# Score bias of the first two batches added by a bf16 matmul instead of on VectorE, with a table that shifts 100 event priorities

## The chip, the cores and the metric

The kernel runs on one core of a Trainium2 chip. The metric is device time in microseconds (us) of one execution, as the median of several runs. Engines are called as in the profile: PE is TensorE, DVE is VectorE, ACT is ScalarE, POOL is GpSimd, SP is SyncE, whose queue issues most of the DMAs.

## The reference: windowed attention, a 2-D Fourier transform and a two-layer network

Inputs are q, k and v of shape (8 batches, 8 heads, 576 positions, 64), and the weights w1 (512 x 2048) and w2 (2048 x 512), which arrive as 64-bit floats.

```python
scores = scale * np.matmul(q, k.transpose(0, 1, 3, 2))
bias = slopes[:, None, None] * (-np.abs(rel))[None]      # slopes 2**-(h+1), rel = position of query - position of key
mask = (rel >= 0) & (rel < 128)
attn = softmax(np.where(mask, scores + bias, -1e9))
x = np.matmul(attn, v)                                   # heads joined: (8, 576, 512)
u = x + np.real(np.fft.fft(np.fft.fft(x, axis=1), axis=2))
un = (u - mean(u)) / sqrt(var(u) + 1e-6)
out = u + np.maximum(un @ w_ch1, 0) @ w_ch2
```

## The kernel before, in words

**Pairs, groups, tiles.** Attention goes by pairs p of heads (four pairs to a batch, so p = 0 to 31). The queries of a pair lie in five tiles, which are taken in three groups (SGRP). A pair's two heads lie on partitions 0 to 63 and 64 to 127, so one head's score matmul uses 64 rows of the PE array. For each group and head a PSUM bank `sp0` or `sp1` is taken from a pool with two of each; the transposes (`turn`) take banks from the same pool.

**The first two batches** (NF = 2, p = 0 to 7) are computed with fp32 matmuls; the later ones split each number into two fp16 halves. For p < 8, `products` issues one fp32 matmul per tile and head (the profile counts each fp32 matmul as two). `spread` then runs one custom DVE instruction per tile and head (L684), which adds the table of distances `rel_sb` times the slope to the scores, writes the result `P` to SBUF and takes the row's extreme into `nb`. DVE is then done with the bank. ACT takes the exponential of `P` in place, `turn` transposes it on PE, ACT copies it out (L718), and `values` multiplies by v (L737). `weigh` divides by the row sums into `X`.

**Fillers.** `warm` (L580) issues PE matmuls whose result nobody reads: SPIN = 5 of them behind each `turn` of the first four pairs, SPIN1 = 1 behind each later one.

**Behind attention.** When all heads of batch b are in `X`, `fourier(b)` folds them on DVE (it begins with a memset of a row of `X`, L801), runs `rows`, `middle` and `cols` on PE and adds the result to `X` (`cols_add`, for j = 1, 0, 2). `norm` takes the statistics of each 128-token tile (bn_stats, L978), a power on POOL, the shift `nmr` on DVE (L983), scales on ACT and sends the result through a transposing DMA to `uT`. `ffn(b)` is the two layers (L1151 and L1173); it is written FFN(0) here for batch 0.

**Side work.** While the first batches run, the weights are loaded, rebuilt from 64-bit words (`rebias`, `join`), measured (`gram`, L466 on PE) and split in two halves (`high`, `low`, L488). `batch_scales(b)` loads a later batch's q, k and v once more into `wall` (`fetch`) to measure them.

**What sets the order.** Every event is put into a queue with a time by hand (`put`); the events are traced in the order of these times. `keep_order` then hands the traced instructions to `arrange`, a list scheduler with its own cost table: on each engine it takes the ready instruction that was traced first. That order is fixed by dependencies, so it is the order in which each engine's instructions stand.

Of the kernel before, what the change touches and what calls it, by code (L numbers as in the profile page):

```python
# [22 lines left out]
NF = 2  # L23
# [23 lines left out]
WL = (-2.569, 0.042)  # L47
PL, VL = 7.393, 1.751
FL, SA, SD, SB, SE = 1.9, 16.181, 0.696, 24.041, 1.166
DFT = 30.695  # L50
START = 47.844
PACE, T1 = (0.507, 0.514), 13.742
SPIN, GAP = 5, 1.315
SLOW = 1.476
W2A, W2D, W2B, W2E = 13.895, 0.615, 21.285, 0.518
W1D, W1B, W1E = 0.379, 11.116, 0.977
F0 = 5.97
SW = 184
SPIN1 = 1
DS, D0 = 1.0, 12  # L60
# [22 lines left out]
WIDTH = {"float32": 4, "float16": 2, "bfloat16": 2, "int32": 4, "int64": 8}  # L83
LANES = ("PE", "DVE", "Activation", "Pool", "SP")
# [28 lines left out]
def cells(a, seen):  # L113
# [4 lines left out]
    if b.tensor.name[:2] in ("fp", "sp", "pv", "pd"):  # L118
        return b.tensor.name, 0, 128, 1
# [16 lines left out]
def nanoseconds(i, lane):  # L136
# [20 lines left out]
    if lane == "Activation":  # L157
        psum = any(a.bass_ap.tensor.name[:2] in ("fp", "sp", "pv", "pd") for a in reads)
        return (58 if psum else 102) + 0.835 * n + 90 * scaled + 190 * (len(i.outs) > 1), False
# [11 lines left out]
def collect(traced):  # L171
    work, seen, last = [], {}, -1
    for at, i in enumerate(traced):
# [21 lines left out]
    writes, reads = {}, {}  # L195
    for n, it in enumerate(work):
        for (t, p0, p1, bits), w in it.uses:
            for l, real in ((writes, True),) + (((reads, False),) if w else ()):
                for m, q0, q1, other in l.get(t, ()):
                    if m != n and q0 < p1 and p0 < q1 and bits & other:  # L200
                        it.waits[m] = it.waits.get(m, False) or real
# [10 lines left out]
def arrange(work, slots):  # L212
# [31 lines left out]
    while len(order) < len(work):  # L244
        best = None
        for e in LANES:
            while now[e] or later[e]:
                t = free[e] if now[e] else max(free[e], later[e][0][0])
                while later[e] and later[e][0][0] <= t:
                    heappush(now[e], heappop(later[e])[1])  # L250
                n = now[e][0]
                t1, tag = buffers(n)
                if t1 is None:
                    held.setdefault(tag, []).append(heappop(now[e]))
                elif t1 > t:
                    ready[n] = max(ready[n], t1)
                    heappush(later[e], (ready[n], heappop(now[e])))
# [5 lines left out]
        n = heappop(now[e])  # L263
# [32 lines left out]
        for m, real in it.then:  # L296
            same = work[m].lane == e
            ready[m] = max(ready[m], end if same and (e == "PE" or not real and e != "SP") else seen + WAKE[work[m].lane])
# [14 lines left out]
def keep_order(tc, slots):  # L313
# [6 lines left out]
    order, takers = arrange(work, slots)  # L320
# [15 lines left out]
def attn_fft_ffn_kernel(  # L336
# [83 lines left out]
    def put(t, f, *a):  # L420
        heappush(queue, (t, next(order), f, a))
# [4 lines left out]

    stage = xp.tile([128, 5, DM], F32, name="X").rearrange("p a b -> p (a b)")
# [85 lines left out]
    def batch_scales(b, t0, dt):  # L513
# [6 lines left out]
        def fetch(x, fl, o, n):  # L520
# [5 lines left out]
            if b > NF:  # L526
                G.tensor_copy(box[x][1][0:1, 0:1], last[-1])
# [124 lines left out]
    def products(p, i):  # L652
        b, j = divmod(p, 4)
        if b < NF:
            prods = ((ops[p][0], ops[p][1]),)
        else:
# [3 lines left out]
        sp = banks[p, i] = [ps_s.tile([128, 512], F32, name=f"sp{e}") for e in range(2)]  # L660
        col = 0
# [10 lines left out]
    def spread(p, i):  # L672
        b, j = divmod(p, 4)
        grp, sp = SGRP[i], banks.pop((p, i))
        P = Ps[p, i] = {}
        for e in range(2):
# [114 lines left out]
    def fourier(b, t0):  # L791
# [161 lines left out]
        for j in (1, 0, 2):  # L953
# [3 lines left out]
            t += f * 0.8  # L957
        put(t0 - 0.1, lambda: uTs.__setitem__(b, []))
# [389 lines left out]
```

## Time and profile before

| What | Value |
|---|---|
| Median of 3 runs | 1042.02 us (1040.59 to 1042.19) |
| The profiled execution | 1041.73 us, span 1039.9 us |
| Mean granted TensorE clock | 0.99 of full speed |
| Busy in the span | PE 97%, DVE 73%, ACT 59%, POOL 7% |

The span runs from the first to the last instruction, and the profiled execution's time is 1.8 us longer. A share of busy time is a mean over stages with different limits. The granted clock has two levels, 1.2 GHz (0.5) and 2.4 GHz (1.0); a value between them is a stretch that held some of each.

### The profile page before, as it was taken

How to read it: one execution, taken by the hardware profiler on the slowest of the kernel's cores; microseconds unless marked ns; L12 is line 12 of the kernel's file. 1: busy time of each engine (PE TensorE's matmuls, PEld its weight loads, DVE VectorE, ACT ScalarE, POOL GpSimd, SP SyncE). 2: the span in 40 equal slices, each digit the busy share in tenths (PEclk: the TensorE clock that was granted, in tenths of full speed). 3: DMA queues.
4: the chain of work that ended last, by engine and by line, in shares of the span. 5: the costliest groups of instructions: out<-in, count | busy, mean ns of one | idle time of the engine just before them, and what ended most of it. 6: DMA issues, size and time to landing. Idle time of an engine off the chain costs nothing.

```text
span 1039.9 us, 24569 instructions
## 1 busy us (share of the span) xinstructions
PE 1006.7 (97%) x9352; PEld 730.7 (70%) x9352; DVE 761.8 (73%) x2211; ACT 609.9 (59%) x1438; POOL 73.3 (7%) x243
## 2 busy tenths in 40 slices
PE   8997799899999999999999999999999999999998
PEld 5785585575767677675767677676767776858886
DVE  5898867986784768778784768779684848987451
ACT  7897967676745566567655566667444532445230
POOL 0000001100210012000000012000000000010000
PEclk9998899999999999999999999999999999999999
DMA  9953517656553366534863376434532230011000
GB/s 365 397 187 95 127 34 197 165 105 152 148 135 87 83 154 145 142 77 121 170 136 90 81 157 146 139 80 103 111 93 33 58 70 11 11 35 39 21 3 30
DMA packets 191511, 117.86 MB, mean 113 GB/s; under 512 B 154400, under 2 KB 164128, under 8 KB 191392
## 3 DMA queue, kind: packets, MB, share of 16 engines
q1 hardware_dynamic: 190816, 114.84, 43.9%
q8 instruction: 73, 1.20, 0.5%
q10 hardware_dynamic: 576, 1.45, 0.4%
q14 instruction: 46, 0.38, 0.1%
HBM read 70.63 MB, written 9.44 MB: 77 GB/s over the span
## 4 chain that ended last, share of the span: by engine, by line
PE 66%; DVE 6%; DMA 3%; ACT 2%; issue 1%; POOL 0%; SPq 0%; ACTq 0%; DVEq 0%; POOLq 0%
PE fp L1151 28%; PE fp L1173 25%; PE fp L1088 4%; PE sp L668 3%; DMA pt<-P 2%; PE pd L871 2%; PE pd L905 1%; PE pv L742 1%; PE pv L744 1%; PE pv L743 1%; DVE hbuf L424 1%; DVE P L684 1%; DMA qr<-q_dram 0%; DVE P L424 0%; PE pd L888 0%
## 5 line engine op out<-in xcount | busy, mean ns | idle before, releaser
L1151 PEld LDWEIGHTS <-wall 128*128 128x128 f16 x3840 | 338.8, 98 | 46.2 <-issue 7.9
L1151 PE MATMUL fp<-uT,wall 128*128 128x256 f16 x3072 | 356.1, 273 | 4.5 <-DVE hbuf L424 4.0
L1173 PE MATMUL fp<-wall,hbuf 128*128 128x512 f16 x1536 | 349.1, 379 | 0.7 <-DVE hbuf L424 0.7
L1173 PEld LDWEIGHTS <-hbuf 128*128 128x128 f16 x1536 | 143.6, 98 | 161.0 <-issue 3.1
L1156 ACT ACTIVATE hbuf<-fp 128x512 f16<-128x512 f32 x144 | 85.0, 591 | 186.7 <-PE fp L1151 186.7
L424 DVE SCALAR_TENSOR_TENSOR hbuf<-fp,hbuf 128x512 f16<-128x512 f32 x144 | 98.7, 686 | 95.0 <-ACT hbuf L1156 94.4
L424 ACT ACTIVATE P<-P,nb 128x256 f32<-128x256 f32 x320 | 132.3, 477 | 13.8 <-DVE nb L684 8.2
L684 DVE CUSTOM_DVE_ANT_0 P<-sp,rg,nsl 128x256 f32<-128x256 f32 x240 | 96.2, 448 | 20.8 <-PE sp L668 15.4
L424 DVE SCALAR_TENSOR_TENSOR P<-P 128x256 f16<-128x256 f32 x240 | 83.0, 389 | 22.2 <-ACT P L697 21.6
L697 ACT ACTIVATE P<-P 128x256 f16<-128x256 f32 x240 | 80.7, 385 | 22.4 <-DMA pt<-P 18.7
L668 PE MATMUL sp<-kk,qq 64*128 64x256 f16 (+5 forms) x880 | 77.3, 287 | 4.1 <-DVE kk L424 3.0
L535 ACT ACTIVATE wall<-wall 128x512 f32<-128x512 f32 (+2 forms) x90 | 54.1, 601 | 35.6 <-DMA wall<-k_dram 17.5
L742 PE MATMUL pv<-vhs,pt 128*128 128x65 f16 x432 | 53.9, 195 | 3.9 <-DMA pt<-P 1.9
L743 PE MATMUL pv<-vl,pt 128*128 128x64 f16 x432 | 53.9, 193 | 0.0
L744 PE MATMUL pv<-vhs,pt 128*128 128x65 f16 x432 | 53.8, 193 | 0.0
L742 PEld LDWEIGHTS <-pt 128*128 128x128 f16 x432 | 41.3, 98 | 16.1 <-issue 4.6
L737 PE MATMUL pv<-vr,pt 128*128 128x65 f32 x288 | 40.7, 281 | 5.6 <-DVE X L760 5.1
L743 PEld LDWEIGHTS <-pt 128*128 128x128 f16 x432 | 40.4, 99 | 7.5
L1151 PE MATMUL fp<-wall,wall 128*128 128x128 f16 x768 | 45.0, 219 | 0.0
L737 PEld LDWEIGHTS pv<-vr,pt 128*128 128x128 f32 x288 | 37.9, 200 | 8.8 <-issue 7.1
L668 PEld LDWEIGHTS <-qq 64*128 64x128 f16 (+1 forms) x720 | 31.1, 99 | 15.4 <-issue 11.7
L744 PEld LDWEIGHTS <-pt 128*128 128x128 f16 x432 | 40.6, 97 | 0.0
(230 smaller groups left out, 1380.5 us busy)
## 6 DMA issues: line engine op xcount, KB each, us to landing
qr<-q_dram SPq DMA_DIRECT2D x32, 304.0 KB, 4.0
hbuf<-w_dram SPq DMA_DIRECT2D x16, 512.0 KB, 8.7
out_dram<-X SPq DMA_DIRECT2D x32, 256.0 KB, 2.2
wall<-v_dram SPq DMA_DIRECT2D x30, 256.0 KB, 3.0
vr<-v_dram SPq DMA_DIRECT2D x24, 320.0 KB, 3.7
kr<-k_dram SPq DMA_DIRECT2D x24, 289.0 KB, 4.4
wall<-q_dram SPq DMA_DIRECT2D x24, 256.0 KB, 3.3
wall<-k_dram SPq DMA_DIRECT2D x24, 256.0 KB, 3.0
```

Source lines behind the costliest of these rows:

```text
L424: put(now[0] + dt, lambda: f(*a, **kw))
L535: A.activation(t, t, AF.Square, accum_out=box["mx"][:, i, c:c + 1])
L668: T.matmul(sp[e][:m, col:col + n], qq[h, c0:c0 + m], keys(kk[h], ti), start=(x == 0), stop=(x == len(prods) - 1))
L684: V.tensor_tensor_reduce(pt[:m, 0:n], sp[e][:m, col:col + n], tab[:m, pc:pc + n], mul, 3.0e38, ALU.add, ALU.min, nb[:m, ti:ti + 1])
L697: A.activation(hi, P32, AF.Copy, scale=2.0 ** 14)
L737: T.matmul(pv[:, ti], pt[:, col:col + 128], ops[p][2][:, e, vc], start=first, stop=last)
L742: T.matmul(pv[:, ti], ph, vh[:, e, vc], start=first, stop=False)
L743: T.matmul(pv[:, ti, 0:D], ph, vl[:, e, vc], start=False, stop=False)
L744: T.matmul(pv[:, ti], pl, vh[:, e, vc], start=False, stop=last)
L1151: T.matmul(fp[:, i * n:(i + 1) * n], w1_ap(e, c, f), uT[:, j, c, 0:n], start=(c == 0 and p == 0), stop=(c == 3 and p == 2))
L1156: A.activation(ht[:, 0], fp, AF.Relu)
L1173: T.matmul(op, hh[f][:, a, i * 128:(i + 1) * 128], w2_ap(e, f), start=(f == 0 and p == 0), stop=(f == 15 and p == 2))
```

## The change

Seven things are changed.

- **Bias on PE.** For p < 8, `products` calls `biased`: per tile and head, a bf16 matmul of `eye` (the 128 x 128 identity times minus the head's slope) with the table `rel_sb` opens the accumulation in the bank, and the fp32 score matmul closes it. The query scale becomes a constant -0.125. `spread` calls `smallest`: DVE only takes the row minimum from PSUM (one instruction for both tiles of the middle group), and ACT takes the exponential straight from PSUM into `P`. A bank is therefore free when ACT has read it. POOL builds the eight `eye` matrices once.
- **Fillers.** SPIN goes from 5 to 1.
- **Statistics.** The first `norm` of a batch is put right behind j = 0 of `cols`, ahead of j = 2. `nmr` is allocated when it is written.
- **Loads.** `fetch` for batches from 3 on loses the POOL copy that made each load wait for the last `weigh`.
- **Scheduler.** `collect` distinguishes three kinds of dependency, and `arrange` sorts ready instructions by a rank.
- **Priorities.** The rank is the event's time plus a shift from `LATER`, a table of 100 named events (the rest have none).
- **Constants.** Some fifteen of the hand-written times change, and three are new.

```diff
-SPIN, GAP = 5, 1.315
+SPIN, GAP = 1, 1.32
...
+LATER = {
+    "W1.load.1": 0.75, "scores.(0,2)+1": 0.15, "W0.gram.3": 12.05, "W0.join.4": 2.8, "W0.gram.6": 2.1,
...
+    eye = att.tile([128, 8, 128], BF16, name="rg", bufs=2)
+    for h in range(8):
+        G.tensor_scalar(eye[:, h], ident, -2.0 ** -(h + 1), None, ALU.mult)
...
-            if b > NF:
-                G.tensor_copy(box[x][1][0:1, 0:1], last[-1])
             nc.sync.dma_start(out=box[x][1], in_=fl[:, o:o + n])
...
-            A.activation(qs, qr, AF.Copy, scale=slope_sb[:, 12 + j:13 + j])
+            A.activation(qs, qr, AF.Copy, scale=-0.125)
...
+        if b < NF:
+            biased(p, i, sp)
+            return
...
+        if b < NF:
+            smallest(p, i, sp)
+            return
...
-                tab, mul = (rel_sb, -2.0 ** -(h + 1)) if b < NF else (scs[b][2], scs[b][1][:m, h:h + 1])
-                V.tensor_tensor_reduce(pt[:m, 0:n], sp[e][:m, col:col + n], tab[:m, pc:pc + n],
-                                       mul, 3.0e38, ALU.add, ALU.min, nb[:m, ti:ti + 1])
+                V.tensor_tensor_reduce(pt[:m, 0:n], sp[e][:m, col:col + n], scs[b][2][:m, pc:pc + n],
+                                       scs[b][1][:m, h:h + 1], 3.0e38, ALU.add, ALU.min, nb[:m, ti:ti + 1])
...
+    def biased(p, i, sp):
+        j, grp = p % 4, SGRP[i]
+        o0 = PCOL[grp[-1]]
+        for ti in grp:
+            c0, pc, n = TILES[ti][0], PCOL[ti], 128 * len(TILES[ti][2])
+            for e in range(2):
+                T.matmul(sp[e][:, pc - o0:pc - o0 + n], eye[:, 2 * j + e], rel_sb[:, pc:pc + n], start=True, stop=False)
+            for e in range(2):
+                h = slice(64 * e, 64 * e + 64)
+                T.matmul(sp[e][:, pc - o0:pc - o0 + n], ops[p][0][h, c0:c0 + 128], keys(ops[p][1][h], ti),
+                         start=False, stop=True)
+
+    def smallest(p, i, sp):
+        grp, P = SGRP[i], Ps[p, i]
+        o0 = PCOL[grp[-1]]
+        for e in range(2):
+            nb = small.tile([128, 5], F32, name="nb", bufs=6)
+            if i == 1:
+                V.tensor_reduce(nb[:, 2:4], sp[e].rearrange("p (a b) -> p a b", a=2), AX.X, ALU.min)
+            for ti in grp:
+                m, o, n = TILES[ti][1], PCOL[ti] - o0, 128 * len(TILES[ti][2])
+                if i != 1:
+                    V.tensor_reduce(nb[:, ti:ti + 1], sp[e][:, o:o + n], AX.X, ALU.min)
+                pt = P[e, ti] = att.tile([128, 256], F32, name="P", bufs=PB)
+                after(0.25, A.activation, pt[:m, 0:n], sp[e][:m, o:o + n], AF.Exp, bias=nb[:m, ti:ti + 1], scale=-1.0)
...
+            if j < 1:
+                put(t - f * 0.1, norm, b, lambda: st["X"][0:2], t + f * N1)
         put(t0 - 0.1, lambda: uTs.__setitem__(b, []))
-        for i, t1 in enumerate((t - f * 0.1, t + f * 0.7)):
-            put(t1, norm, b, lambda i=i: st["X"][2 * i:2 * i + 2], t + f * (0.9 + 1.6 * i))
+        put(t + f * N2, norm, b, lambda: st["X"][2:4], t + f * N3)
```

The table and the scheduler move instructions on every engine. Two places show it. The first is PE in the second pair of heads, around the `values` of its second group (`x3` is three alike; `kk,qq` are scores, `ident,P` transposes, `vr,pt` values, `pv<-pt` fillers). Before:

```order
L668 MATMUL sp_582<-kk,qq 96x256
L715 MATMUL sp_605<-ident,P 128x128 x3
L737 MATMUL pv<-vr,pt 128x65 x3
L580 LDWEIGHTS pt
L580 MATMUL pv<-pt 128x184
...
L715 MATMUL sp_632<-ident,P 128x128 x3
L737 MATMUL pv<-vr,pt 128x65 x4
```

Where the line of dots stands, the filler comes four more times. Now:

```order
L746 MATMUL sp_567<-rel_sb,rg 128x256
L749 MATMUL sp_566<-kk,qq 128x256
L749 MATMUL sp_567<-kk,qq 128x256
L627 LDWEIGHTS pt
L627 MATMUL pv<-pt 128x184
L790 MATMUL sp_594<-ident,P 128x128 x3
...
L812 MATMUL pv<-vr,pt 128x65 x3
```

A bias matmul on all 128 rows (`rel_sb,rg`) now stands between score matmuls on 64 rows, one filler stands where five stood, and the dots leave out a `gram`.

The second place is DVE at the first statistics of batch 0 (`un` of FFN(0) needs `nmr`). Before, both halves' statistics are gathered, and the six instructions of `cols_add` for j = 2 lie behind the first of four bn_stats:

```order
L978 BN_STATS st<-X 128x6
L923 TENSOR_TENSOR ds<-ab 33x257
L924 TENSOR_TENSOR ds<-ab 33x256
L931 TENSOR_TENSOR ds<-ab 32x257
L930 TENSOR_TENSOR X<-X,ds 1x512
L932 TENSOR_TENSOR ds<-ab 32x255
L933 TENSOR_TENSOR ut<-X,ds 32x512
L934 TENSOR_TENSOR ut<-X,ds 32x512
L979 BN_AGGR ag<-st 128x2
L978 BN_STATS st<-X 128x6 x2
```

Now:

```order
L1054 BN_STATS st<-X 128x6 x2
...
L1056 TENSOR_SCALAR rstd<-ag 128x2
L998 TENSOR_TENSOR ds<-ab 33x257
L835 TENSOR_TENSOR X<-pv,ri 128x5x64
L999 TENSOR_TENSOR ds<-ab 33x256
L1006 TENSOR_TENSOR ds<-ab 32x257
L1005 TENSOR_TENSOR X<-X,ds 1x512
L1007 TENSOR_TENSOR ds<-ab 32x255
L1008 TENSOR_TENSOR ut<-X,ds 32x512
L1009 TENSOR_TENSOR ut<-X,ds 32x512
L1062 SCALAR_TENSOR_TENSOR nmr<-ag,rstd 128x2
```

The first half's two bn_stats and its variance now stand ahead of the additions of j = 2, but the shift `nmr` still stands behind them, and the second half's bn_stats have gone behind `nmr`.

## Rows read from the trace of the kernel before

**Rows 1.** The page: busy us (share of the span) of each engine.
```profile
PE 1006.7 (97%) x9352; PEld 730.7 (70%) x9352; DVE 761.8 (73%) x2211; ACT 609.9 (59%) x1438; POOL 73.3 (7%) x243
```

**Rows 2.** Busy by stretch: start:end, length, PE, PEld, DVE, ACT, POOL, PEclk, DMA share, GB/s.
```profile
0.00:122.00 122.00, 105.99 (x845) 80.60 (x846) 100.58 (x329) 100.23 (x223) 3.54 (x21) 0.93 0.69 242
122.00:312.00 190.00, 181.15 (x1620) 127.55 (x1619) 148.43 (x445) 129.59 (x312) 23.28 (x68) 0.99 0.56 133
312.00:1040.00 728.00, 719.54 (x6892) 522.50 (x6889) 512.79 (x1439) 380.12 (x904) 46.44 (x154) 1.00 0.38 87
```

**Rows 3.** The same view of three stretches ahead of and into FFN(0).
```profile
8.00:76.00 68.00, 65.43 (x575) 52.44 (x572) 59.81 (x203) 61.59 (x130) 0.12 (x1) 1.00 0.88 329
80.00:92.00 12.00, 9.10 (x36) 5.51 (x37) 11.94 (x39) 7.99 (x15) 0.31 (x3) 0.57 0.04 10
116.00:125.00 9.00, 8.36 (x39) 6.18 (x39) 6.38 (x16) 9.00 (x17) 0.11 (x1) 0.52 0.65 146
```

**Rows 4.** PE's waits in 0 to 122 us: total us, times, longest us.
```profile
PE sp L715 <- ACT P L424: 5.6, 3, 4.0
PE pv L737 <- DVE X L760: 4.6, 1, 4.6
...
PE sp L668 <- ACT pt L718: 0.5, 1, 0.5
```

**Rows 5.** PE in order of time: start us, us, instruction, count.
```profile
11.97 0.70 PE L668 MATMUL sp<-kk,qq 64*128 64x256 f32 x2
12.60 0.40 PE L466 MATMUL fp<-wall 128*128 128x128 bf16 x4
...
24.66 0.57 PE L580 MATMUL pv<-pt 128*128 128x184 bf16 x5
25.07 1.03 PE L737 MATMUL pv<-vr,pt 128*128 128x65 f32 x8
...
41.69 0.70 PE L668 MATMUL sp<-kk,qq 64*128 64x256 f32 x4
42.32 0.60 PE L715 MATMUL sp<-ident,P 96*128 96x96 f32 x4
...
50.19 1.13 PE L668 MATMUL sp<-kk,qq 64*128 64x256 f32 x8
51.25 0.55 PE L715 MATMUL sp<-ident,P 128*128 128x128 f32 x3
...
121.66 6.86 PE L1151 MATMUL fp<-uT,wall 128*128 128x256 f16 x48
129.16 16.01 PE L1151 MATMUL fp<-uT,wall 128*128 128x256 f16 x144 [0.64 <-DVE hbuf L424]
```

**Rows 6.** DVE in order of time, the same columns.
```profile
67.62 0.41 DVE L684 CUSTOM_DVE_ANT_0 P<-sp,rel_sb 128x256 f32<-128x256 f32 x1
...
67.96 0.41 DVE L684 CUSTOM_DVE_ANT_0 P<-sp,rel_sb 96x256 f32<-96x256 f32 x1
...
73.26 0.48 DVE L801 MEMSET X<- 1x512 f32 x1
...
99.63 0.42 DVE L684 CUSTOM_DVE_ANT_0 P<-sp,rel_sb 128x256 f32<-128x256 f32 x1 [2.93 <-PE sp L668]
...
103.46 0.28 DVE L470 TENSOR_REDUCE wm<-fp 128x1 f32<-128x128 f32 x1
103.66 0.48 DVE L760 TENSOR_TENSOR X<-pv,ri 128x320 f32<-128x320 f32 x1
...
113.36 0.15 DVE L983 SCALAR_TENSOR_TENSOR nmr<-ag,rstd 128x2 f32<-128x2 f32 x1
```

**Rows 7.** ACT by form, 8 to 76 us: count, busy us, mean ns, idle before.
```profile
L424 ACT ACTIVATE P<-P,nb 128x256 f32<-128x256 f32 x28 | 13.8, 498 | 1.1 <-DVE nb L684 1.1
```

**Rows 8.** PE's waits from 122 us on, the columns of group 4.
```profile
PE fp L1151 <- DVE hbuf L424: 4.0, 6, 1.5
PE sp L668 <- DVE kk L424: 3.0, 2, 2.4
```

More of the change, by code (lines that the diff above doesn't have):

```diff
@@ L1 @@
+from bisect import bisect_right
 from contextlib import ExitStack
@@ L157, in nanoseconds @@
     if lane == "Activation":
-        psum = any(a.bass_ap.tensor.name[:2] in ("fp", "sp", "pv", "pd") for a in reads)
+        psum = any(a.bass_ap.tensor.name[:2] in BANKS for a in reads)
         return (58 if psum else 102) + 0.835 * n + 90 * scaled + 190 * (len(i.outs) > 1), False
@@ L194, in collect @@
             it.cost.append(nanoseconds(i, lane))
-    writes, reads = {}, {}
+    writes, reads, firsts = {}, {}, {}
     for n, it in enumerate(work):
+        for (t, *_), _ in it.uses:
+            m = firsts.setdefault(t, n)
+            if m != n and work[m].lane == it.lane:
+                it.waits.setdefault(m, 0)
         for (t, p0, p1, bits), w in it.uses:
-            for l, real in ((writes, True),) + (((reads, False),) if w else ()):
+            for l, real in ((writes, 2), (reads, 1)):
                 for m, q0, q1, other in l.get(t, ()):
+                    if real == 1 and not w and (work[m].lane == it.lane or t[:2] not in BANKS):
+                        continue
                     if m != n and q0 < p1 and p0 < q1 and bits & other:
-                        it.waits[m] = it.waits.get(m, False) or real
+                        it.waits[m] = max(it.waits.get(m, 0), real)
         for (t, p0, p1, bits), w in it.uses:
@@ L297, in arrange @@
             same = work[m].lane == e
-            ready[m] = max(ready[m], end if same and (e == "PE" or not real and e != "SP") else seen + WAKE[work[m].lane])
+            at_end = same and (e == "PE" or not real or real == 1 and e != "SP")
+            ready[m] = max(ready[m], end if at_end else seen + WAKE[work[m].lane])
             open_[m] -= 1
@@ L319, in keep_order @@
     work = collect(list(tc.nc.cur_bb.bb.instructions))
-    order, takers = arrange(work, slots)
+    starts = [0] + [m[0] for m in marks]
+    times = [-1.0e9] + [m[1] for m in marks]
+    order, takers = arrange(work, slots, [times[bisect_right(starts, it.at) - 1] for it in work])
     last = {}
@@ L418, in attn_fft_ffn_kernel, with put @@
     now = [0.0]
-    def put(t, f, *a):
-        heappush(queue, (t, next(order), f, a))
+    scope, here, seen, marks = [""], [""], {}, []
+    def put(t, f, *a, name=None):
+        base = here[0] + "+" if here[0] else scope[0] + f.__name__ + "".join(
+            "." + str(x).replace(" ", "") for x in a if type(x) in (int, tuple))
+        base = name or base
+        seen[base] = seen.get(base, 0) + 1
+        key = base + str(seen[base]) if base.endswith("+") else base if seen[base] == 1 else f"{base}#{seen[base]}"
+        heappush(queue, (t, next(order), key, f, a))
     def after(dt, f, *a, **kw):
         put(now[0] + dt, lambda: f(*a, **kw))
+    eye = att.tile([128, 8, 128], BF16, name="rg", bufs=2)
+    for h in range(8):
+        G.tensor_scalar(eye[:, h], ident, -2.0 ** -(h + 1), None, ALU.mult)
     stage = xp.tile([128, 5, DM], F32, name="X").rearrange("p a b -> p (a b)")
@@ L972, in norm @@
         uTs[b].append(uT)
+        nmr = []
         ag = small.tile([128, 4, 2], F32, name="ag")
         rstd = small.tile([128, 4], F32, name="rstd")
-        nmr = small.tile([128, 4], F32, name="nmr")
         for i, t in enumerate(tiles):
@@ L1216, in step @@
             t += dt + (E0 if steps[0] == 16 else 0.0)
-            put(t, step, g, t, dt)
+            put(t, step, g, t, dt, name=f"step{steps[0]}")
     for b in range(B):
```

62 lines of the change are left out of this document (36 added, 26 removed), and 21 rows, old and new, of the table LATER.

## The prediction

> **What bounds the kernel now.** I read the page first: PE is busy for 97% of the span, no other engine for more than 73%, and POOL for 7% [rows 1]. So the time is the sum of what PE has to do, plus what it loses idle or at the low clock, and the question is where it loses. The busy time by stretch answers that [rows 2]: in 0 to 122 us PE is idle for 16.0 us and the granted clock is 0.93; from 122 to 312 us it is idle for 8.9 us; from 312 us to the end for 8.5 us. Since 122 us is where FFN(0) begins (121.66) [rows 5], the first stage holds half of all idle time and all of the low clock.
>
> Then three closer stretches [rows 3]. In 8 to 76 us PE is busy for 65.4 of 68 us, ACT for 61.6 and DVE for 59.8: three engines are nearly full at once, but PE's share holds fillers. In 80 to 92 us DVE is full (11.9 of 12), PE is busy for 9.1 at a clock of 0.57; in 116 to 125 us PE is busy for 8.4 at 0.52. PE's waits name what stood ahead of these falls [rows 4]: one wait of 4.0 us for an exponential, while DVE folded batch 0 for the transform, and one of 4.6 us for `X`, while DVE finished the transform and the statistics. At 0.57 and 0.52 some 9.1 x 0.43 + 8.4 x 0.48 = 7.9 us were lost to the clock. From 122 us on, PE's longest waits are for `hbuf` (4.0 us in 6) and for the converted keys (3.0 in 2) [rows 8].
>
> **The prices.** From one start to the next [rows 5]: five fillers take 25.07 - 24.66 = 0.41 us, so 0.082 each. One fp32 score matmul of 256 columns takes 12.60 - 11.97 = 0.63, two for the two heads side by side also 42.32 - 41.69 = 0.63, four 51.25 - 50.19 = 1.06. So a run of score matmuls costs 0.20 fixed and 0.43 for each step, and a lone one costs as much as a pair. A 16-bit matmul of 256 columns takes 16.01 / 144 = 0.111, and half that for 128.
>
> **The change part by part: PE.** Counted in the order, fillers go from 144 to 48: -96 x 0.082 = -7.9 us. Added are 64 + 16 bias matmuls: 64 x 0.111 + 16 x 0.056 = +8.0 us. No row shows a matmul with `eye`; between 0, if it only filled idle time, and 0.27 each (the length of one that is not overlapped, which would make 22 us), I take 0.111, since it has the shape and type of that row. The 80 fp32 score matmuls stay, but a bias matmul now stands between them: they stood in 39 runs and stand in 62, and 44 are alone. Priced by steps and runs they go from 28.1 to 36.1 us, +8.0, of which the fixed part is 23 x 0.20 = 4.6. PE's own work therefore grows by 8.0 + 8.0 - 7.9 = 8.1 us.
>
> The Trainium skill bears on the fixed part: TensorEngine Tiling (Array Packing), section Key Properties, says that changing the tiling mode, here from 64 rows to 128, drains TensorE; it names no price. It speaks against this change, since each bias matmul that stands alone asks for two switches. Without any price for a switch the sum below would be 4.6 us lower.
>
> **Where that work lies.** Counted ahead of FFN(0)'s first matmul, the new order holds 74 of the 80 score matmuls instead of 70, with 74 bias matmuls (+7.3), 24 more runs (+8.9 in all), ten more transposes and five more value matmuls (about 0.11 and 0.22 each from the 0.60 and 1.03 us of four [rows 5]: +2.2) and 94 fewer fillers (-7.7): +10.7 us ahead, and so 10.7 - 8.1 = 2.6 us less behind. The stage had 16.0 us idle and 7.9 us lost to the clock: some 24 us, from which those 10.7 can be taken.
>
> **When FFN(0) starts.** Batch 0's last value matmuls have almost the same priced work ahead of them on PE as before (+0.5 us: bias +4.7, runs +3.2, `gram` work moved ahead +0.6, fillers -7.9). So `fourier(0)` begins 0.5 us later than at 73.26 [rows 6]; if PE waits more, up to 4 us. From there DVE sets the pace until `nmr` at 113.36: 40.1 us, with one wait of 2.9 for scores [rows 6]. DVE's part of the bias edit is worth little: a custom instruction of 256 columns takes 67.96 - 67.62 = 0.34 us, of 128 columns about 0.2, and a plain reduce of 128 columns also 103.66 - 103.46 = 0.20. Only the 16 merged pairs save some 0.08 each, 1.3 us in the whole stage. No reduce of 256 from PSUM is shown; between 0.27 (no fixed part) and 0.42 (the row's length) I take the custom's 0.34. The early statistics are worth little too: `nmr` still stands behind the six additions of j = 2, and only two bn_stats (0.6 each, an estimate from two customs of 256) and small ones leave the chain; one weighing and one `low` come in. Priced row by row that part shrinks by 1.0 us; the wait of 2.9 may or may not stay. I take -2.0 (-3.9 to 0). The way from `nmr` to the first matmul, 8.3 us (scaling, transposing DMA), stays. FFN(0) starts 0.5 - 2.0 = -1.5 us from before; range -3.5 to +4.
>
> **Costed at nothing.** The eight `eye` matrices lie on an idle POOL ahead of the first scores; uncovered, they would cost at most the start. The constant query scale and the exponential from PSUM leave ACT about as long as the 0.498 us of rows 7; ACT is not full, and any gain is hidden behind DVE. The POOL copies ahead of the later loads go; POOL is 7% busy, and what the loads do without them counts with the waits below.
>
> **The sum**, against the profiled execution's 1041.73 us: start of FFN(0) -1.5; less work behind it -2.6; the clock at its start -1.0 (before, 121.66 to 125 ran at the low level, worth 1.7 us; range -1.7 to +1); the waits from 122 us on -1.5. PE was idle there for 8.9 + 8.5 = 17.4 us, part of it at the very end, where nothing changes, and the new order is different almost everywhere; nothing in the trace says which waits go, so I take a tenth or less and keep -5 to +3. Together -6.6: 1035.1, and against the median of 1042.02, 0.3 above the profiled run, **1035.4 us**. Its own range is 1030 to 1040.
>
> **The rivals.**
> - *Both low-clock stretches and most later waits go.* Fillers of real work stand where PE waited 4.0 and 4.6 us, and the order was shifted over the whole program. Start -3.5, behind -2.6, clock -1.7, waits -5: -12.8, 1029.2. For it: the new order has more PE work ahead of the transform's `rows`. Against it: DVE stays full in that stretch.
> - *PE becomes the bound ahead of FFN(0).* It is 96% busy in 8 to 76 us already [rows 3], and fillers could be idle time in disguise while bias matmuls can't. If half of the 10.7 us isn't covered, FFN(0) starts 4 us later: 4 - 2.6 - 1 = +0.4, 1042.4. If no wait went at all it would be the full +8.1.
> - *Banks are held too long: slower.* A score bank used to be free after DVE, and PE waited for banks next to nothing (0.5 us for a transposed copy [rows 4]). Now it is free only after ACT's exponentials, of 0.5 us each [rows 7], on an ACT that is 91% busy, and the first bias matmul of a group waits for them. There are 48 such takes. At 0.25 us each PE loses 12.0 us in the stage that feeds `fourier(0)`: -6.6 + 12.0 = +5.4, 1047.4. It decides from 6.6 / 48 = 0.14 us a take.
> - *The clock falls earlier.* The stretch from 8 to 76 us ran at 1.00 with fillers in every gap [rows 3]; two more falls like those would cost 7.9 us: -6.6 + 7.9 = +1.3, 1043.3. The Trainium skill, TensorE: Matmul & The Clock Gate, section What's actually happening, says that the low clock is the default and activity lifts it; by that rule the filler's loss matters only where nothing takes its place.
>
> **How the numbers follow.** Chances: the forecast 0.50, the larger gain 0.17, PE as the bound 0.13, banks 0.15, the clock 0.05. The measurement can tell about 0.2% (2.1 us) from no change. The forecast and the larger gain are faster: 0.67. PE as the bound and the clock count as no change: 0.18. The banks are slower: 0.15. The range reaches to beyond the larger gain at its bound of waits and almost to the banks' time: 1026 to 1046.
>
> **What would show it.** PE's waits in 0 to 122 us show the banks: a wait of a bias matmul for an exponential of over 7 us in total is that rival. The first FFN matmul's start, 120.2 by the sum, shows the stage, and the memset of `fourier(0)` and `nmr` at 73.8 and 111.9 its two halves. The clock in 76 to 125 us shows the falls. PE's idle time behind that start, 17.4 us before, shows the rest. Starts of lone score matmuls 0.63 us apart confirm the price of a run. The prediction fails if FFN(0) starts after 126 us, or if the later waits double.

## The result, and the profile after

The changed kernel takes 1025.17 us (median of 4 runs, 1022.85 to 1027.48); the kernel before took 1041.91 us (4 runs). The ratio is 0.984, 95% interval 0.982 to 0.986: 16.7 us faster. The prediction was 1035.4 us, 1026 to 1046: the side is right, the time lies just below the range.

The page of the changed kernel, the line that answers to [rows 1] (the span is 1024.1 us, the profiled execution's time 1025.91):

```profile
PE 1006.4 (98%) x9336; PEld 725.7 (71%) x9336; DVE 764.4 (75%) x2115; ACT 610.1 (60%) x1438; POOL 51.5 (5%) x176
```

In this execution PE is busy as long as before, but at full speed all the time. The busy time by stretch shows it, in the columns of [rows 2, 3]:

```profile
0.00:122.00 122.00, 117.27 (x894) 82.83 (x895) 103.93 (x255) 100.48 (x230) 7.75 (x29) 1.00 0.68 240
117.40:122.00 4.60, 4.60 (x45) 4.12 (x43) 3.71 (x8) 4.60 (x10) 0.00 (x0) 1.00 0.36 78
117.40:312.00 194.60, 186.83 (x1734) 135.13 (x1732) 153.47 (x447) 138.00 (x333) 8.00 (x46) 1.00 0.65 145
312.00:1024.00 712.00, 706.85 (x6755) 511.91 (x6753) 510.66 (x1422) 376.24 (x886) 35.76 (x101) 1.00 0.38 85
8.00:76.00 68.00, 67.58 (x521) 48.31 (x518) 59.98 (x149) 59.63 (x131) 0.12 (x1) 1.00 0.87 329
80.00:92.00 12.00, 9.96 (x91) 6.49 (x91) 11.97 (x27) 8.11 (x22) 0.10 (x1) 1.00 0.01 1
116.00:125.00 9.00, 8.18 (x76) 7.31 (x76) 7.16 (x12) 9.00 (x18) 0.11 (x1) 1.00 0.64 156
```

The clock is 1.00 in the two stretches where it was 0.57 and 0.52. Two timelines, the columns of [rows 5, 6]: PE at places that the prediction priced, then DVE at the two marks of the first stage.

```profile
80.47 0.39 PE L746 MATMUL sp<-rel_sb,rg 128*128 128x256 bf16 x2
80.79 0.70 PE L749 MATMUL sp<-kk,qq 64*128 64x256 f32 x4
81.43 0.41 PE L515 MATMUL fp<-wall 128*128 128x128 bf16 x4
...
96.94 0.27 PE L746 MATMUL sp<-rel_sb,rg 128*128 128x256 bf16 x1
97.15 0.70 PE L749 MATMUL sp<-kk,qq 64*128 64x256 f32 x2
97.77 0.23 PE L746 MATMUL sp<-rel_sb,rg 128*128 128x128 bf16 x1
97.93 0.49 PE L749 MATMUL sp<-kk,qq 64*128 64x128 f32 x2
...
117.40 0.82 PE L1231 MATMUL fp<-uT,wall 128*128 128x256 f16 x6
```

```profile
71.49 0.48 DVE L876 MEMSET X<- 1x512 f32 x1
...
107.77 0.16 DVE L1062 SCALAR_TENSOR_TENSOR nmr<-ag,rstd 128x2 f32<-128x2 f32 x1
```

`fourier(0)` begins at 71.49 (73.26 before), `nmr` stands at 107.77 (113.36), FFN(0) starts at 117.40 (121.66). PE's waits ahead of that start, and the first of those behind it (columns of [rows 4]):

```profile
PE pv L623 <- POOL stack L413: 1.5, 1, 1.5
PE sp L790 <- ACT P L470: 1.1, 2, 0.8
PE fp L946 <- ACT fh L919: 1.0, 1, 1.0
PE fp L946 <- DVE fl L931: 0.6, 1, 0.6
...
PE fp L1231 <- DVE hbuf L470: 3.6, 4, 1.7
PE fp L1231 <- DVE X L470: 1.9, 1, 1.9
```

The waits of 4.0 and 4.6 us [rows 4] are gone, and no bias matmul waits for an exponential.

**Where the time went.** Against before's span of 1039.9, four pieces make the 15.8 us. FFN(0) starts 4.3 earlier. Behind that start PE was busy for 901.0 us, 1.5 of them lost at half clock, and now for 186.83 + 706.85 = 893.7: 5.8 us less work and 1.5 less lost. And it was idle there for 918.2 - 901.0 = 17.2 us, now for 906.7 - 893.7 = 13.0: 4.2 less. Ahead of the start PE's work at full speed grew from about 99 to 117.27 - 4.60 = 112.7 us, while idle and lost time there fell from some 22 us to 4.7. Over the whole span idle time fell from 1039.9 - 1006.7 = 33.2 us to 1024.1 - 1006.4 = 17.7, which is more than what the clock gave back.

### The profile page after: what moved, and what is told of

It is laid out like the page before. It is cut to its first block, busy times and chain, and to the rows that moved or that the text cites. A ratio compares the mean times of both kernels' runs of the same rounds, so it can differ in the third digit from the quotient of the medians.

```text
span 1024.1 us, 24257 instructions
## 1 busy us (share of the span) xinstructions
PE 1006.4 (98%) x9336; PEld 725.7 (71%) x9336; DVE 764.4 (75%) x2115; ACT 610.1 (60%) x1438; POOL 51.5 (5%) x176
## 4 chain that ended last, share of the span: by engine, by line
PE 82%; DVE 10%; ACT 4%; DMA 2%; issue 1%; SPq 0%; POOL 0%; DVEq 0%; ACTq 0%; POOLq 0%
PE fp L1231 33%; PE fp L1253 27%; PE fp L1168 4%; PE sp L716 3%; PE pd L946 2%; DMA pt<-P 2%; PE sp L749 2%; PE pv L812 2%; PE pd L980 1%; PE pv L817 1%; PE pv L819 1%; PE pv L818 1%; PE sp L790 1%; ACT P L470 1%; DVE wall L470 1%
## 5 line engine op out<-in xcount | busy, mean ns | idle before, releaser
L470 DVE SCALAR_TENSOR_TENSOR hbuf<-fp,hbuf 128x512 f16<-128x512 f32 x144 | 99.0, 687 | 79.6 <-ACT hbuf L1236 78.3
L470 ACT ACTIVATE P<-P,nb 128x256 f32<-128x256 f32 (+1 forms) x240 | 99.3, 480 | 19.3 <-DVE nb L734 19.0
L817 PE MATMUL pv<-vhs,pt 128*128 128x65 f16 x432 | 52.6, 195 | 1.7 <-DMA pt<-P 1.1
L819 PE MATMUL pv<-vhs,pt 128*128 128x65 f16 x432 | 52.2, 193 | 0.0
L716 PE MATMUL sp<-kk,qq 64*128 64x256 f16 (+2 forms) x720 | 42.8, 260 | 0.1
L1070 ACT ACTIVATE un<-X,nmr,rstd 128x512 f32<-128x512 f32 x32 | 25.7, 809 | 26.9 <-DVE nmr L1062 24.9
L749 PE MATMUL sp<-kk,qq 64*128 64x256 f32 (+1 forms) x160 | 41.2, 407 | 0.0
```

The source lines that it names most:

```text
L470: put(now[0] + dt, lambda: f(*a, **kw))
L716: T.matmul(sp[e][:m, col:col + n], qq[h, c0:c0 + m], keys(kk[h], ti), start=(x == 0), stop=(x == len(prods) - 1))
L749: T.matmul(sp[e][:, pc - o0:pc - o0 + n], ops[p][0][h, c0:c0 + 128], keys(ops[p][1][h], ti), start=False, stop=True)
L817: T.matmul(pv[:, ti], ph, vh[:, e, vc], start=first, stop=False)
L819: T.matmul(pv[:, ti], pl, vh[:, e, vc], start=False, stop=last)
```

## The experiments

Two kinds of kernel were run. In the first five the planner (`arrange`) orders the edited program anew. In the others the order of every engine is held: the program is planned as it was, and then built with the edit in that order. "Lost" is PE's busy time times (1 - granted clock), summed over windows of 20 us to 140 us and of 40 us to 300, of the profiled execution: 8.6 us before, 0 in the changed kernel. It differs from one execution to the next, and before's profiled execution is a mild one: its mean granted clock is 0.990, while 65 executions of the same kernel that ran beside the experiments have 0.980 to 0.990, with a median of 0.985 (the changed kernel: 0.996 to 1.000 in four).

| Kernel | Median (range), us | Ratio to before, 95% | fourier(0) | FFN(0) | Lost |
|---|---|---|---|---|---|
| a_notable | 1050.8 (1050.7 to 1051.3) | 1.0069 to 1.0104 | 72.7 | 125.6 | 16.2 |
| a_dvebias | 1038.1 (1036.8 to 1041.0) | 0.9955 to 0.9980 | 65.7 | 118.4 | 17.6 |
| a_tied | 1033.7 (1033.4 to 1034.7) | 0.9902 to 0.9945 | 70.9 | 118.3 | 5.9 |
| a_late | 1041.0 (1037.2 to 1042.5) | 0.9975 to 1.0002 | 71.3 | 119.3 | 4.0 |
| a_nudge | 1042.9 (1041.9 to 1045.9) | 1.0012 to 1.0035 | 71.6 | 126.6 | 14.5 |
| b_hold | 1047.5 (1041.6 to 1052.9) | 1.0026 to 1.0085 | 73.8 | 128.6 | 13.5 |
| b_fill1 | 1042.5 (1038.9 to 1044.2) | 0.9997 to 1.0022 | 71.8 | 120.2 | 11.3 |
| f_beye | 1048.1 (1046.8 to 1048.7) | 1.0047 to 1.0078 | 78.3 | 127.2 | 8.5 |
| a_fill5 | 1035.0 (1033.5 to 1036.4) | 0.9915 to 0.9955 | 78.5 | 125.9 | 3.0 |
| f_dve | 1039.8 (1036.0 to 1046.6) | 0.9955 to 1.0012 | 79.6 | 133.2 | 26.7 |
| f_dve0 | 1027.4 (1026.4 to 1028.9) | 0.9857 to 0.9886 | 72.1 | 120.8 | 3.3 |
| f_dve5 | 1039.9 (1034.9 to 1047.8) | 0.9978 to 1.0031 | 76.6 | 126.8 | 10.9 |
| f_late | 1032.7 (1031.5 to 1034.4) | 0.9891 to 0.9939 | 71.3 | 125.2 | 7.9 |
| a_fill0 | 1023.9 (1023.5 to 1025.1) | 0.9810 to 0.9853 | 69.9 | 116.8 | 1.6 |
| f_pair2 | 1025.2 (1024.4 to 1026.4) | 0.9821 to 0.9865 | 70.5 | 117.9 | 1.6 |

### One part undone, planned anew

**a_notable**: no table.

```diff
-LATER = { ... }
+LATER = {}
```

> The changed kernel with an empty table of priorities; everything else stays. Theory (the order did it: the table puts TensorE's work where it waited): most of the 16.7 us gain goes, 1036 to 1042 us, FFN(0) starts after 120 us, and TensorE has a stretch at a granted clock near 0.5 between 76 and 125 us. Rival (the bias matmuls did it: they keep TensorE busy wherever they stand): within 4 us of the changed kernel's 1025.2, the clock at 1.00 throughout and FFN(0) at 117 to 119 us.

25.6 us over the changed kernel, more than the theory asked for and slower than before.

**a_dvebias**: `biased` and `smallest` out, the query scale, `products` and `spread` as before.

> The changed kernel with the distances of the two fp32 batches added on VectorE again, as before the change; table, one filler, statistics and loads stay. TensorE's own work falls by about 21 us (13.4 of bias matmuls, 7.8 of score runs). Theory (the order did it, and the bias matmuls are a cost that was hidden or paid): 1015 to 1030 us. Rival (the bias matmuls did it): at least 1034 us, with the clock falling to 0.5 between 76 and 125 us, because nothing fills TensorE's waits there.

1038.1 us: `fourier(0)` begins 5.8 us earlier, and 17.6 us are lost at half clock. These are the rival's numbers, and a first sign against the theory that the bias matmuls only cost.

**a_tied**: the copy back.

```diff
+            if b > NF:
+                G.tensor_copy(box[x][1][0:1, 0:1], last[-1])
             nc.sync.dma_start(out=box[x][1], in_=fl[:, o:o + n])
```

> The changed kernel with the tie of the later loads put back: a copy on GpSimd ahead of each load of batches 3 to 7, which waits for the last weighed head. Theory (loads were hidden anyway): within 2 us of 1025.2, idle time of TensorE behind FFN(0)'s start 13 us as now. Rival (the ties made the later waits, and their going is the 4.2 us less of idle time there): 3 to 5 us slower, 1028 to 1030, and as much more idle time behind FFN(0)'s start; FFN(0) itself starts at 117.4 under both.

8.5 us slower, more than either. New waits of values for a transposing DMA (4.3 us) and for `X` (3.8) stand behind FFN(0)'s start, and half-clock stretches with them; how much of that is the tie and how much the other order can't be told from it.

**a_late**: both `norm` events at before's times.

```diff
-            if j < 1:
-                put(t - f * 0.1, norm, b, lambda: st["X"][0:2], t + f * N1)
...
-        put(t + f * N2, norm, b, lambda: st["X"][2:4], t + f * N3)
+        for i, t1 in enumerate((t - f * 0.1, t + f * 0.7)):
+            put(t1, norm, b, lambda i=i: st["X"][2 * i:2 * i + 2], t + f * (0.9 + 1.6 * i))
```

> The changed kernel with both halves' statistics at the places they had before the change, behind the last additions. Theory (the early statistics are a small part): the first shift nmr, now at 107.8 us, comes 1 to 2 us later, FFN(0) too, and the time is 1026 to 1028 us. Rival (they are the main part of the 5.6 us by which nmr came earlier): nmr at 111 us or later, FFN(0) after 120 us, 1029 us or more.

The time is the rival's, its place is not: in the profiled execution (the fastest of ten) `nmr` comes only 1.0 us later and FFN(0) 1.9; the other 9.3 us come behind that start.

All four lost much, whatever was undone. So the next question was what any other order costs.

**a_nudge**: one constant of the planner.

```diff
-PACE, T1 = (0.507, 0.514), 13.742
+PACE, T1 = (0.507, 0.515), 13.742
```

> The changed kernel with one constant of the planner moved by 0.2% (the pace of batch 0's transform, 0.514 to 0.515), so that the same instructions come out in an order that differs in places. Theory (the order was chosen for this program alone, and any new planning of it loses several us): 1028 to 1036 us. Rival (small changes of the order are worth little, and what a_tied, a_late and a_dvebias lost comes from the part that was undone): within 2 us of 1025.2.

17.7 us, all of the gain, for 0.2% of one pace; the theory had expected 3 to 11. PE, in two windows of it, and its longest wait there:

```profile
100.00:108.00 8.00, 7.44 (x46) 4.38 (x45) 7.84 (x21) 6.63 (x23) 1.04 (x2) 1.00 0.62 191
108.00:129.00 21.00, 20.07 (x87) 16.26 (x88) 13.49 (x37) 15.67 (x31) 1.80 (x2) 0.51 0.47 92
...
PE pv L812 <- DVE X L835: 1.1, 1, 1.1
```

PE was busy for 7.4 of 8 us ahead of the fall, which came inside a wait of 1.1 us for `X`, and then for 20.1 of 21 us at half speed: the clock took 9.8 us there, and FFN(0) started 9.2 later. So a kernel that is planned anew says little about the part that was undone, and the rest was done with the order held.

### The clock, the fillers and PE's work, with the order held

**b_hold**: before, with fillers in its two long waits.

```diff
+KEEP = {(4, 1, 1): (46, "turn", (4, 2, 0)), (5, 2, 0): (50, "values", (5, 0, 1))}
...
+        for _ in range(KEEP.get(key, (0,))[0]):
+            HOLD[len(tc.nc.cur_bb.bb.instructions)] = key
+            T.matmul(spare_cols["pv"], rel_sb[:, 0:128], rel_sb[:, 0:SW], start=True, stop=True)
```

> The kernel before, its order unchanged, with 46 and 50 more filler matmuls put where TensorE waited 4.0 us (at 78 us) and 4.6 us (at 111 us). Both theories expect the granted clock at 1.00 from 76 to 125 us. Theory (what TensorE lost at half clock, 8.3 us, is lost to the time as a whole): 1033 to 1035 us. Rival 1 (the first fall lies behind a full VectorE, and only the second, 2.5 us ahead of FFN(0) and 1.5 behind its start, counts): 1037 to 1038.5 us, nmr at 113.4 us as before. Rival 2 (both are hidden): within 1.5 us of the kernel before.

The theory and the first rival failed on what they shared, the clock at 1.00, and 1047.5 us is outside all three ranges. PE's rows and two windows of b_hold:

```profile
78.34 3.80 PE L589 MATMUL pv<-rel_sb 128*128 128x184 bf16 x46
82.53 0.44 PE L725 MATMUL sp<-ident,P 128*128 128x128 f32 x2 [0.39 <-ACT P L430]
...
115.39 6.29 PE L589 MATMUL pv<-rel_sb 128*128 128x184 bf16 x50
```

```profile
80.00:84.00 4.00, 3.14 (x32) 2.41 (x29) 3.94 (x12) 2.39 (x4) 0.21 (x2) 1.00 0.00 0
84.00:88.00 4.00, 3.69 (x18) 1.90 (x17) 4.00 (x9) 1.87 (x4) 0.10 (x1) 0.72 0.00 0
```

The wait is filled, and the clock falls all the same, some 5 us later, in a stretch of fp32 transposes, scores and values with waits under 0.5 us. It fell again ahead of the second filling, which then ran mostly at half speed (6.29 us for 50, against 3.80 for 46) and made PE late. Long waits alone don't explain the falls. This execution is one of the two slowest of eight, with a mean clock of 0.982; three others had 0.993 to 0.995 and still took 1041.6 to 1043.5 us, no less than the kernel before. A higher clock, got in this way, did not bring the gain.

**b_fill1** (before, one filler for five) and **a_fill5** (changed, five for one):

```diff
-        for _ in range(n if "pv" in spare_cols else 0):
+        for _ in range((1 if n == SPIN else n) if "pv" in spare_cols else 0):
```

```diff
+        for _ in range(more if "pv" in spare_cols else 0):
+            FILL.add(len(tc.nc.cur_bb.bb.instructions))
+            T.matmul(spare_cols["pv"], x[:, 0:128], x[:, 0:SW], start=True, stop=True)
```

> The kernel before, its order unchanged, with one filler in place of five: 96 fillers fewer, 8 to 9 us of TensorE work by their starts. Theory (they are real work where TensorE is full, 8 to 76 us): fourier(0) begins 3 to 8 us ahead of 73.3 us, and the time falls by 2 to 6 us. Rival (they only fill waits): fourier(0) within 1 us of 73.3, the time within 2 us, or later if the clock falls in 8 to 76 us.

> The changed kernel, its order unchanged, with five fillers again where it has one: 96 more, 8 to 9 us of TensorE work. Theory (TensorE is the bound ahead of FFN(0) in the changed kernel: 4.7 us idle in 117): FFN(0) starts 5 to 9 us after 117.4 us, and the time is 1030 to 1034 us. Rival (VectorE sets the pace there, and TensorE's work is covered): FFN(0) within 2 us of 117.4, the time within 3 us of 1025.2.

In the old order 96 fillers fewer bring 1.4 us at `fourier(0)` (0.4 more than the rival allowed) and nothing at the end; the rival holds. In the changed kernel the same 96 cost 7.0 us at `fourier(0)`, 8.5 at FFN(0) and 9.8 in all (1 us over the theory's range): PE has no room left there. Between the two marks lies a stretch at half clock, 94 to 98 us, that took 1.7 us.

**f_beye**: before, with bias matmuls of a zero matrix.

```diff
+                    extra(T.matmul, sp[e][:m, col:col + n], eye[:, 0:m], rel_sb[:, PCOL[ti]:PCOL[ti] + n],
+                          start=True, stop=False)
```

> The kernel before, its order unchanged, with 80 more matmuls of the bias matmuls' shape, of a zero matrix, each ahead of its score matmul; VectorE still adds the distances. This is some 13 us of TensorE work (80 x 0.167) and nothing else. Theory (in the old order bias matmuls are a cost, and the gain is the new order's): fourier(0) 5 to 10 us later than 73.3 us and the time 5 to 11 us longer. Rival (they fill waits and hold the clock up): within 2 us of the kernel before or faster, with the clock at 1.00 in 76 to 125 us.

As the theory said: `fourier(0)` 5.0 us later, and 7.2 us in all against the 1040.85 us of the kernel before beside it. In the old order bias matmuls cost time, and the clock gains little: 8.5 us are lost in the profiled execution, and the mean clock of four executions is 0.989, beside 0.984 without them.

**f_dve**: the changed kernel's order without bias matmuls, distances on VectorE.

```diff
-            for e in range(2):
+            for e in range(0 if RUN[0] else 2):
                 T.matmul(sp[e][:, pc - o0:pc - o0 + n], eye[:, 2 * j + e], rel_sb[:, pc:pc + n], start=True, stop=False)
...
+                    V.tensor_tensor_reduce(pt[:m, 0:n], src, rel_sb[:m, PCOL[ti]:PCOL[ti] + n],
+                                           -2.0 ** -(2 * (p % 4) + e + 1), 3.0e38, ALU.add, ALU.min, nb[:m, ti:ti + 1])
```

> The changed kernel, its order unchanged on every engine, with the distances of the fp32 batches added on VectorE again and no bias matmuls: some 13 us of bias matmuls and part of 7.8 us of score runs less on TensorE, a custom instruction for each reduce on VectorE. Theory (TensorE's work is the bound in the stage ahead of FFN(0), so bias matmuls there cost time, and the clock was held by the order): fourier(0) 3 to 8 us ahead of 71.5 us, the time 1012 to 1022 us. Rival (in this order the bias matmuls are what holds the clock up): stretches at half clock are back between 76 and 125 us, over 8 us long, and the time is 1025 to 1037 us.

**f_dve0**: the same, but the bias matmuls stay, of a zero matrix.

```diff
-        G.tensor_scalar(eye[:, h], ident, -2.0 ** -(h + 1), None, ALU.mult)
+        G.tensor_scalar(eye[:, h], ident, 0.0 if RUN[0] else -2.0 ** -(h + 1), None, ALU.mult)
```

> The changed kernel's order on every engine, bias matmuls of a zero matrix where the bias matmuls stand, and the distances added on VectorE (custom instructions in place of the reduces). TensorE has all the work of the changed kernel, VectorE that of the kernel before. Theory (the bias matmuls hold the clock up as 16-bit work among fp32 work): no stretch at half clock of more than 4 us ahead of 125 us, the time 1024 to 1029 us. Rival (VectorE's lighter work keeps TensorE fed): long stretches at half clock as in f_dve, 1034 us or more.

The two differ only in 80 matmuls whose result is zero. f_dve's theory failed: `fourier(0)` came 8.1 us later and not earlier. The rival's stretches are there, ahead of 76 us too, and the time is 2.8 us above its range. Two windows of f_dve with the waits at their start and all waits of that kind in 0 to 125 us, then the same windows of f_dve0 and its waits in 8 to 100 us:

```profile
22.00:36.00 14.00, 13.24 (x60) 10.07 (x60) 8.96 (x29) 9.21 (x20) 0.00 (x0) 0.51 1.03 406
...
70.00:94.00 24.00, 24.00 (x108) 18.96 (x108) 17.21 (x52) 13.44 (x27) 0.21 (x2) 0.51 0.17 55
...
22.76 0.31 PE L695 MATMUL pv<-pt 128*128 128x184 bf16 x1 [1.32 <-DVE X L912]
69.68 0.24 PE L695 MATMUL pv<-pt 128*128 128x184 bf16 x1 [1.32 <-DVE X L912]
...
PE pv L695 <- DVE X L912: 5.1, 4, 1.5
```

```profile
22.00:36.00 14.00, 14.00 (x108) 10.13 (x106) 12.73 (x43) 12.55 (x30) 0.00 (x0) 1.00 1.03 406
...
70.00:94.00 24.00, 21.63 (x174) 14.71 (x172) 23.54 (x70) 17.84 (x43) 0.31 (x3) 1.00 0.18 50
...
PE pv L695 <- DVE X L910: 0.2, 1, 0.2
```

Without them PE is busy for all of 24 us at half clock; with them the clock is up. 12.5 us lie between the two kernels, and only 2.2 between f_dve0 and the changed kernel: in this order the bias matmuls are worth more for what they put on PE than for what they take from VectorE. How they hold the clock is not shown. They are 16-bit work on all 128 rows among fp32 work; but with them the four waits for `X` are next to nothing, and two of these stand where f_dve's long falls begin. No run has the one without the other. In one point f_dve0's theory was too strict: a stretch of 6.8 us at half clock was left, at 115 us.

**f_dve5**: f_dve with five fillers behind each transpose.

```diff
+            for k in range(4 if RUN[0] and n == -1 else 0):
+                EXTRA[len(tc.nc.cur_bb.bb.instructions)] = 1 + k
+                T.matmul(spare_cols["pv"], x[:, 0:128], x[:, 0:SW], start=True, stop=True)
```

> The changed kernel's order, no bias matmuls, the distances on VectorE, and five fillers again where the changed kernel has one (96 more, 8.9 us of 16-bit work). Theory (any 16-bit work there holds the clock): of the 28 us lost at half clock in f_dve less than 10 are left, the time 1018 to 1030 us. Rival (fillers stand behind the transposes, not among the score matmuls, and don't hold it): more than 15 us lost, 1034 us or more.

The time is the rival's, the loss lies between the two: 10.9 us in the fastest of ten executions. Over all of them the mean clock has a median of 0.982, against 0.973 in f_dve. The waits for `X` are almost as long as there (4.0 us in four in 8 to 100 us). So fillers behind the transposes hold the clock in part without taking the waits away; how large a part stays open.

### Statistics, fillers and runs in the changed kernel, with the order held

**f_late**: batch 0's first statistics moved behind the additions of j = 2, right ahead of `nmr`.

> The changed kernel, its order unchanged but for batch 0's first-half statistics on VectorE, which stand right ahead of nmr, behind the additions of j = 2, as before the change. Theory (only the instructions that left the chain count): nmr 1.8 to 3 us after 107.8 us, FFN(0) as much later, the time 1027 to 1028.5 us. Rival (something else is last ahead of FFN(0)): FFN(0) within 0.7 us of 117.4.

`nmr` comes at 111.5 (+3.7; 1.6 us of that were lost at half clock in 80 to 100), FFN(0) at 125.2 (+7.8). PE's wait of f_late in 100 to 126 us, and its windows there:

```profile
PE sp L876 <- DVE un L556: 3.4, 1, 3.4
```

```profile
100.00:113.00 13.00, 12.04 (x86) 8.69 (x84) 10.58 (x28) 8.98 (x27) 0.81 (x2) 1.00 0.39 134
113.00:127.00 14.00, 11.60 (x48) 7.92 (x49) 11.31 (x31) 12.77 (x27) 0.80 (x2) 0.52 0.49 119
```

3.7 us on VectorE became a wait of 3.4 us on PE, the clock fell, and PE's work up to and into FFN(0) took 11.60 x 0.48 = 5.6 us longer. `nmr` fits the theory once the 1.6 us are taken off, the time does not. The early statistics are worth up to 7.5 us in this order; the fall in 80 to 100 us lies ahead of the instructions that were moved, and a_fill0 and f_pair2 have one there too.

**a_fill0** (no fillers at all) and **f_pair2** (bias, bias, score, score together):

```diff
     def warm(x, n):
+        if RUN[0] and "pv" in spare_cols:
+            return
```

```diff
+        mine = sorted((x for x in xs if x.name in GROUP), key=lambda x: GROUP[x.name][1])
+        for (n, _), x in zip(pe[at:end], mine + [x for x in xs if x.name not in GROUP]):
+            seq[n] = x
```

> The changed kernel, its order unchanged, without its 48 fillers (39 ahead of FFN(0), 0.093 us each, 3.6 us). Theory (TensorE is the bound ahead of FFN(0)): FFN(0) 2 to 4 us ahead of 117.4, the time 1021 to 1023.5 us. Rival (the fillers hold the clock up): stretches at half clock ahead of 125 us, the time 1027 us or more.

> The changed kernel with one move on TensorE alone: where the bias and score matmuls of the two heads of a group are separated only by each other, by fillers or by gram, they stand together as bias, bias, score, score. Ten runs of score matmuls fewer, and more pairs side by side. Theory (a run costs 0.20 us fixed and a lone score matmul as much as a pair): 2 to 4 us less work on TensorE, fourier(0) 1 to 3 us ahead of 71.5 us, the time 1021 to 1024 us. Rival (the second head's bank isn't free yet, or the clock falls): new waits of bias matmuls for an exponential, the time 1025 us or more.

Neither can be told from the changed kernel, though 1023.9 us is the shortest median. Both have a short half-clock stretch at 85 us. a_fill0 fits neither side: `fourier(0)` comes 1.6 us earlier, FFN(0) 0.6. PE in 8 to 76 us of f_pair2, and its longest waits there (L837 is the bias matmul):

```profile
8.00:76.00 68.00, 63.17 (x529) 46.45 (x526) 60.61 (x152) 60.39 (x133) 0.12 (x1) 1.00 0.88 329
...
PE sp L837 <- ACT P L559: 3.2, 5, 1.2
```

PE has 4.4 us less work than in the changed kernel, a little more than the 2 to 4 that the price of a run gave, but it became idle time. That is the rival: bias matmuls now wait for exponentials, because the second head's bank isn't free yet. Added work costs nearly in full (a_fill5), removed work brings nothing at the end.

## Why the prediction was wrong in size

**The step that failed** is the account of the 24 us that PE lost ahead of FFN(0), idle or at half clock. It let 10.7 us of new work lie there and 1.5 us come back; the runs show some 13.5 us of work and 4.3 us. With the later waits, where it took 1.5 us and 4.2 went, that is nearly all of the 9 us between forecast and result: more idle time went than it allowed, and the new work was covered. Four rows show it on the way to `nmr`, in the columns of [rows 2]: before, up to `fourier(0)` and from there to `nmr`; then the same now.

```profile
0.00:73.26 73.26, 69.23 (x572) 52.63 (x573) 57.14 (x196) 61.03 (x129) 1.53 (x13) 1.00 0.87 322
73.26:113.36 40.10, 30.96 (x254) 23.48 (x250) 36.81 (x104) 30.76 (x81) 1.22 (x6) 0.87 0.38 118
...
0.00:71.49 71.49, 69.60 (x511) 47.94 (x512) 55.56 (x138) 58.14 (x126) 5.62 (x21) 1.00 0.89 336
71.49:107.77 36.28, 34.24 (x278) 24.39 (x279) 35.59 (x84) 28.41 (x77) 1.33 (x6) 1.00 0.31 89
```

Up to `fourier(0)` PE's work grew by 0.4 us, as forecast, and its idle time fell from 4.0 to 1.9. From there to `nmr` DVE's work fell by 1.2 us (forecast 1.0), but its idle time from 3.3 to 0.7: the wait of 2.9 us for scores [rows 6], which the prediction left open and counted at about a third, went whole. So "From there DVE sets the pace until `nmr`" was not all of it. Before, PE was 4.0 us behind by its stretch at half clock (80.3 to 90.5 us), worked on without a wait over 0.5 us from 82 to 99 us, and DVE then waited for its scores: the first fall was not fully covered.

- **PE's own work, +8.1.** Measured +8.3 with the table's loss (1006.4 against 1006.7 less 8.6), or 13.5 - 5.8 = +7.7 by the pieces above, whose windows are cut finer. The pieces of the forecast were off in part. A bias matmul takes 0.21 us ahead of a score matmul and two take 0.32, not 0.111 each: by an estimate some 5 us more for the 80, which other pieces made good that the rows don't show one by one. The 0.63 us of a lone score matmul stands (97.15 to 97.77). Fillers cost a little less than forecast (a_fill5: 7.0 us at `fourier(0)` for 7.9).
- **fourier(0), +0.5.** It came 1.8 us earlier. f_beye shows that in the old order the bias matmuls alone put it 5.0 us later; the new order took them with 2.1 us less idle time.
- **`nmr`, -2.0.** The way there shrank by 3.8 us (40.1 to 36.3), almost the bound of -3.9 that the prediction gave for the case that the wait goes.
- **nmr to FFN(0), 8.3 us unchanged.** It took 9.6; the runs don't say why.
- **The early statistics, "worth little".** By rows they are 2 us; in f_late their loss cost up to 7.5, through a wait and the clock.
- **Work behind FFN(0), -2.6; the clock at its start, -1.0; later waits, -1.5.** Measured -5.8, -1.5 and -4.2. All but 0.5 of the 5.8 us of work lie ahead of 303 us; 2.6 is what the count of moved matmuls gave, and the rest isn't assigned. For the waits the prediction said that nothing in the trace tells which go. The 3.0 us for converted keys [rows 8] are gone, and 3.1 of the 4.2 lie in one stretch, 357 to 537 us before and 345 to 521 now (idle 3.5 and 0.4); none of the runs settles which entries of the table took them.
- **The rivals.** "Both low-clock stretches and most later waits go" (1029.2): both stretches went, and the time is another 4 us shorter, but of the 17.2 us of later waits only 4.2 went (the rival took 5). What stood against it came true and did not matter: DVE stays full in 80 to 92 us. "Banks are held too long" is refuted by the waits. "PE becomes the bound" is right in that PE has no room left now (a_fill5), and wrong of the cost, since the new work was covered. "The clock falls earlier" did not happen in the changed kernel's profiled execution, and in the old order one filler for five changed the mean clock by nothing that can be told (b_fill1: median 0.9835 in ten executions, beside 0.984).

How much of the gain is the clock's stays open. In the profiled executions idle time fell by 15.5 us and the loss by 8.6. Among the 65 executions of the kernel before, the 16 with a mean clock of 0.983 or less took 1041.6 us on average and the 21 with 0.987 or more 1040.5: 1.1 us apart, where the mean clock times the span gives 5.6 us, so what differs between them was mostly covered. In f_late and a_nudge it wasn't: FFN(0) started 7.8 and 9.2 us later. The prediction tied the two falls to the two long waits; b_hold shows a fall without one, f_dve and f_dve0 that the same order runs at either level by 80 16-bit matmuls, and a_nudge that a small change of the order brings 14.5 us of loss. The bias matmuls need the order and the order needs them: with the old order they cost 7.2 us, without them the new order gains next to nothing (1039.8), with both it is 16.7. The old order with bias matmuls and one filler for five, as the change has them together, wasn't run. What stays open, besides how the bias matmuls hold the clock, is which of the 100 entries and new constants matter, and what the untied loads are worth by themselves: no run ties them again with the order held.

The Trainium skill, TensorE: Matmul & The Clock Gate, section What's actually happening, says that activity releases the throttle. The kernel before agrees: its two falls stand at waits of 4.0 and 4.6 us [rows 4]. f_dve does not: PE was busy for 24.0 of 24 us, as the profile counts it, at a clock of 0.51.

## What to carry to other kernels

Look at the granted clock of each stretch and at what work stood ahead of a fall, not only at waits: in this kernel's new order 80 16-bit matmuls between fp32 ones held the clock, where 96 fillers behind the transposes did so in part. Take it from several executions, since one profile can be a mild one. To learn what one part of a change is worth, hold the order of all engines and take only that part out; a planner that ran anew moved the time by 8 to 26 us in each of five edits, even in one that did nothing else. And where a delay can cost the clock, price it with the stretch behind it at half speed, not by its own length.

## What was not expected of the hardware

PE ran at half clock with every one of 24 us busy (f_dve, 70 to 94 us), and fell to it in a wait of 1.1 us behind 7.4 us busy of 8 (a_nudge). In a_tied PE's instructions and waits from 80 to 86 us are those of the changed kernel, 0.6 us earlier, and behind them the clock fell for 3.4 us in the one and not in the other. Some kernels that lose much at half clock scatter by 1% from one execution to the next (f_dve 1036.0 to 1046.6 us, b_hold 1041.6 to 1052.9), and their time goes with the mean clock (f_dve: 0.977 at 1036.0, 0.964 at 1046.6); others scatter less (a_dvebias, 1036.8 to 1041.0 in ten). The changed kernel scatters by 0.5%.
